# The last 64 rows of three weight matrices loaded in another shape, and two wo heads loaded apart

## The chip, the core and the metric

One core of one Trainium2 chip runs the kernel. The metric is the device time of one execution in microseconds; before the change three runs took 1284.09, 1285.81 and 1285.73 us (median 1285.73). The profile is of one further execution. A core has engines that run side by side, each with its own queue of instructions: TensorE (PE, with its weight loads shown as PEld), VectorE (DVE), ScalarE (ACT), GpSimd (POOL) and SyncE (SP), which here issues nearly all transfers. The transfers themselves run on 16 DMA engines. Engines wait for each other through semaphores.

## The reference, cut to what matters

One token of decoding: 16 query heads of 256 over 8 key/value heads with 65536 cached positions, a gated feed-forward block on the same x, and a mix of the two by a gate.

```python
x = A_x                                            # 1 x 1 x 448
g = sigmoid((x * gate_w).sum(-1, keepdims=True))
q = (x @ wq)                                       # wq 448 x 4096, 16 heads of 256
p = softmax(q . k / 16)                            # per head, over 65536 positions
o = p @ v                                          # two query heads share one k/v head
a = o.reshape(1, 1, 4096) @ wo                     # wo 4096 x 448
gate, up = x @ W_gate, x @ W_up                    # 448 x 1792 each
b = (gate * (gate > 0) * up) @ W_down              # W_down 1792 x 448
out = g * a + (1 - g) * b
```

All tensors are bfloat16. The K and V caches are 268 MB each, everything else together about 12 MB.

## The kernel before

A planner object collects operations (`op`), transfers (`dma`) and operations that use one shared PSUM bank (`mop`). Each has an engine, a key and the operations it depends on. `finish` sorts every engine's list by key, and that is the order in which the engine's queue runs; `emit` puts a semaphore wait in front of an operation for each dependency. A transfer counts as done when its semaphore has risen by 16, so a wait on it is for the whole transfer. The keys are estimated due times: `order` lists the loads in the order of issue with a length for each (`TILE` 19.35 for an 8.4 MB tile of K or V), and `tL` holds the running sum.

Loads go into three large SBUF buffers, `ring[0..2]`, in rotation. Each of the 8 k/v heads has four K tiles and four V tiles, 32 of each. The order is: wq and the main parts of W_gate and W_up, the last rows of wq, the first K tile, the last rows of W_gate and W_up, W_down, then K and V tiles in turn, V three tiles behind. Heads 0 to 2 of wo come after V tile 29, head 3 after V tile 30; the last V tile comes in four pieces (`PIECES`, half, quarter, eighth, eighth), and then heads 4, 5, 7 and 6 of wo, head 6 in two halves (`WOP`, L211). W_down and the second K tile wait until q is computed, because they overwrite wq's buffers.

A K tile is transposed by VectorE in eight pieces (L351), multiplied with q by TensorE (L363), reduced to a maximum by VectorE (L502) and exponentiated by ScalarE (L504). Behind the fourth tile of a head stand the maximum over all tiles, the rescaling (L524) and TensorE's transposes of the probabilities (L529). A V tile is multiplied by them (L397). When a head is complete, VectorE copies o (L411, L412), TensorE turns it into columns with eight small products (L420), VectorE scales them (L427), and `f_wo` (L594) multiplies them with that head's part of wo into one accumulator, eight products for a head. The last step copies the accumulator (L603) and stores it (L605).

A matrix of 448 rows doesn't fill 128 partitions evenly. The first 384 rows are loaded three to a partition in one transfer (wq L436, W_gate and W_up L450). `rows64` (L371) loads the last 64 rows of each of the three matrices: eight transfers of 6 rows (L374) on partitions 0 to 23 and 32 to 55 of one buffer, and four transfers of 4 rows (L377) on partitions 0 to 15 of a second one; the rows of one transfer lie four partitions apart. Partitions of the first buffer that hold no row are set to zero beforehand (`z_q` on VectorE, L243, for wq; `z_f` on GpSimd, L244, for the other two), and the transfers wait for it. x is brought into the matching arrangement by small products (`f_xT`, L289) and copies (`f_xT2`, L298); `xw` spreads it so that a product puts q of one head into one row of PSUM. `f_q` (L311) computes q from the first 384 rows; `f_q2` (L318) adds the last 64, with 16 products over 56 partitions (L320) and 16 over 16 (L323). `f_gu` (L454) and `f_gu2` (L464) do the same for W_gate and W_up, with 28 products over 56 partitions (L468) and 28 over 16 (L473) in `f_gu2`.

At the end the keys of the last wo products hang on `t7` (L587), the key of the last head's scaling L427: heads 4 and 5 get `t7 - 0.6`, ahead of the small products L420 (`t7 - 0.5`), the others `t7 + 0.6`.

Of the kernel before, what the change touches and what calls it, by code (L numbers as in the profile page):

```python
# [90 lines left out]
def bass_gated_mix__gqa_block_cached__glu_gated_reglu__decode_kernel(  # L91
# [13 lines left out]
    H = A_k_cache.shape[1]  # L105
# [13 lines left out]
    NX = R3 + 2  # L119
    KA = 48  # L120
    KB = D - NR3 - KA
# [6 lines left out]
    assert KR == 64 and KB == 16 and FT * 128 == F and FT <= 14 and FT % 2 == 0 and D <= 448 and H >= 3  # L128

    es = ExitStack()  # L130
    with es:
# [29 lines left out]
        xw = P_sb[:, 0:NX * 160]  # L161
        iot = P_sb[:, 800:1056].bitcast(I32)
        qn = P_sb[:, 1056:1312]
        x_row = P_sb[0:1, 1312:1312 + D]
        fin_o = P_sb[0:1, 0:D]
# [5 lines left out]
        wqa, wqb = ring[1][:, 0:NQ], ring[1][:, NQ:2 * NQ]  # L171
# [35 lines left out]
        for n in range(1, NT):  # L207
            order.append(("k", n, TILE))
            if n >= NTH - 1:
                order.append(("v", n - (NTH - 1), TILE))  # L210
        WOP = [[(0, 0, 4), (1, 0, 4), (2, 0, 4)], [(3, 0, 4)],  # L211
               [(4, 0, 4), (5, 0, 4), (7, 0, 4), (6, 0, 2), (6, 2, 4)]]
# [30 lines left out]
        z_q = op("dv", -0.5, lambda e: e.memset(wqa[0:32, :], 0.0))  # L243
        z_f = op("gp", -0.5, lambda e: e.memset(ring[2][0:32, R3 * NQ + 2 * R3 * F:R3 * NQ + 2 * R3 * F + 2 * F], 0.0))  # L244
        c_xT = op("dv", -0.3, lambda e: e.memset(xT[:], 0.0))
# [43 lines left out]
        def f_xT(e):  # L289
            for kt in range(R3):  # L290
                e.matmul(XT_ps[:, kt:kt + 1], x_row[0:1, kt:NR3:R3], one_t[0:1, 0:1], start=True, stop=True)
            for p0 in (0, 32):
                c0 = NR3 + (p0 // 32) * 24
                e.matmul(XT_ps[p0:p0 + 24, R3:R3 + 1], x_row[0:1, c0:c0 + 24], one_t[0:1, 0:1], start=True, stop=True)
            return e.matmul(XT_ps[0:KB, R3 + 1:NX], x_row[0:1, NR3 + KA:D], one_t[0:1, 0:1], start=True, stop=True)
        x1_ = mop("pe", 0.6, f_xT, [d_x, c_o1])

        def f_xT2(e):  # L298
            e.tensor_copy(xT[:, 0:R3], XT_ps[:, 0:R3])
            for p0 in (0, 32):  # L300
                e.tensor_copy(xT[p0:p0 + 24, R3:R3 + 1], XT_ps[p0:p0 + 24, R3:R3 + 1])
            return e.tensor_copy(xT[0:KB, R3 + 1:NX], XT_ps[0:KB, R3 + 1:NX])
        x2_ = mop("dv", 0.7, f_xT2, [x1_, c_xT])


        xw3 = xw.rearrange("p (kt c) -> p kt c", kt=NX)
        def f_xw(e):
            return e.tensor_copy(xw3[:, :, 31:160:32], xT[:].unsqueeze(2).to_broadcast([128, NX, 5])[:, :, 0:5])
# [9 lines left out]
        def f_q2(e):  # L318
            for j in range(J):
                e.matmul(QN_ps, xw3[0:56, R3, 31 - j:159 - j], wqa[0:56, j * 256:(j + 1) * 256],  # L320
# [323 lines left out]
```

## Time and profile before

| | us |
|---|---|
| three runs | 1284.09, 1285.81, 1285.73; median 1285.73 |
| the profiled execution | 1284.16 |
| its span, first to last instruction | 1282.9 |
| busy in it: VectorE | 638.9 (50%) |
| TensorE products | 430.9 (34%) |
| TensorE weight loads | 163.2 (13%) |
| ScalarE | 61.4 (5%) |
| GpSimd | 7.6 (1%) |

The profile divides the span into 40 equal slices and gives each engine's busy share in tenths, the share of the 16 DMA engines, and the rate at which they moved data. A group line gives line, engine, operation and tiles, the count, the total and mean time, and then the time the engine had stood idle before these instructions with what ended it. A timeline line gives start, length, engine, line, operation, tiles and count; the bracket at its end is the idle time ahead of it and its releaser. A line marked SPq is a transfer being issued, not its way through the DMA engines. A row of a table of windows gives start and end, the length, and for each of five engines busy time and (in brackets) count, then the clock granted to TensorE, the DMA share and GB/s. The lines on the sizes of transfers end with the time from issue to landing.

### The profile page before, as it was taken

What the parts mean: (1) busy time and instruction counts of PE and PEld (TensorE: products, weight loads), DVE (VectorE), ACT (ScalarE), POOL (GpSimd) and SP (SyncE); (2) the same over time, 40 slices, a digit from 0 to 9 for tenths busy, and PEclk for the clock granted to TensorE, in tenths of its full rate; (3) what the DMA queues carried; (4) which work ended last, traced back from release to release, by engine and by line L of the source; (5) the groups of instructions that cost most, each with busy time, mean ns of one, the idle gap of its engine ahead of it and who ended that gap; (6) DMA issues with size and microseconds to landing.
All of it is one profiled execution on the core that took longest, in us unless ns stands there. A gap on an engine that the chain in (4) does not pass through costs nothing.

```text
span 1282.9 us, 10059 instructions
## 1 busy us (share of the span) xinstructions
PE 430.9 (34%) x4649; PEld 163.2 (13%) x4649; DVE 638.9 (50%) x439; ACT 61.4 (5%) x116; POOL 7.6 (1%) x22
## 2 busy tenths in 40 slices
PE   5424423334223431225331343321433323233245
PEld 3301101111001110002110111100111101011011
DVE  2588633565434655445555444555434655335600
ACT  0000000000000000000000000000000000000000
POOL 2000000000000000000000000000000000000000
PEclk8665666656666666666656676656566656666566
DMA  9999999999999999999999999999999999999997
GB/s 413 436 426 430 438 434 426 438 435 432 428 434 436 436 430 429 432 444 426 426 440 438 425 434 440 428 425 438 440 426 430 436 439 426 436 430 438 432 399 317
DMA packets 11904, 549.68 MB, mean 428 GB/s; under 512 B 1427, under 2 KB 1686, under 8 KB 2710
## 3 DMA queue, kind: packets, MB, share of 16 engines
q1 hardware_dynamic: 11858, 549.03, 99.2%
q8 instruction: 36, 0.59, 0.2%
q14 instruction: 6, 0.05, 0.0%
q10 hardware_dynamic: 4, 0.00, 0.0%
HBM read 549.03 MB, written 0.00 MB: 428 GB/s over the span
## 4 chain that ended last, share of the span: by engine, by line
DVE 35%; DMA 31%; another core or an unknown queue 16%; PE 15%; SPq 2%; issue 1%; ACT 1%
DVE ring L351 31%; DMA ring<-in_A_k_cache_dram 27%; PE ST L363 6%; PE O L397 6%; DMA ring<-in_A_wo_dram 3%; DVE P_sb L524 1%; DMA ring<-in_B_W_up_dram 1%; SPq L374 1%; DVE nmb L502 1%; PE PT L529 1%; SPq L377 1%; ACT ptp L538 0%; PE M_ps L516 0%; DVE attnT L427 0%
## 5 line engine op out<-in xcount | busy, mean ns | idle before, releaser
L351 DVE STREAM_TRANSPOSE ring<-ring 128x2048 uint32<-128x2048 uint32 x256 | 565.5, 2275 | 405.8 <-DMA ring<-in_A_k_cache_dram 405.8
L363 PE MATMUL ST<-ring,xm 128*16 128x512 bf16 x2048 | 224.7, 612 | 755.7 <-DVE ring L351 755.7
L363 PEld LDWEIGHTS ST<-ring,xm 128*16 128x16 bf16 x2048 | 62.2, 120 | 904.3 <-DVE ring L351 796.2
L397 PE MATMUL O<-ring,ptp 128*4 128x512 bf16 x2048 | 150.9, 458 | 32.7 <-DMA ring<-in_A_v_cache_dram 28.7
L504 ACT ACTIVATE P_sb<-ST,nmb 128x512 bf16<-128x512 f32 x32 | 45.1, 1410 | 1107.8 <-DVE nmb L502 1107.8
L502 DVE TENSOR_REDUCE nmb<-ST 128x1 f32<-128x512 f32 x32 | 22.1, 689 | 109.3 <-PE ST L363 109.3
L397 PEld LDWEIGHTS O<-ring,ptp 128*4 128x4 bf16 x2048 | 54.9, 99 | 127.8 <-issue 60.4
L411 DVE CAST o_sb<-O 128x512 bf16<-128x512 f32 x8 | 5.5, 692 | 77.0 <-PE O L397 77.0
L524 DVE TENSOR_TENSOR P_sb<-P_sb,hs 128x1024 bf16<-128x1024 bf16 x16 | 18.9, 1222 | 8.7 <-ACT hs L518 8.7
L529 PE MATMUL PT<-identb,P_sb 128*128 128x128 bf16 x128 | 16.5, 310 | 15.5 <-DVE P_sb L524 14.7
L529 PEld LDWEIGHTS PT<-identb,P_sb 128*128 128x128 bf16 x128 | 12.3, 140 | 18.3 <-DVE P_sb L524 18.3
L538 ACT COPY ptp<-PT 128x256 bf16<-128x256 bf16 x32 | 10.4, 376 | 23.0 <-PE PT L529 23.0
L442 DVE STREAM_TRANSPOSE ptp<-P_sb 128x128 uint32<-128x128 uint32 x1 | 0.3, 311 | 18.3 <-ACT P_sb L441 18.3
L504 ACT ACTIVATION_READ_ACCUMULATOR P_sb<-ST,nmb 128x1 f32 x32 | 8.4, 262 | 0.0
L314 PE MATMUL M_ps<-ring,P_sb 128*128 128x256 bf16 x48 | 7.1, 322 | 0.8 <-DMA ring<-in_A_wq_dram 0.8
L427 DVE TENSOR_SCALAR attnT<-M_ps,hs 64x4 bf16<-64x4 f32 x16 | 3.5, 221 | 5.4 <-PE M_ps L420 5.3
L514 PE MATMUL M_ps<-identf,hs 128*2 128x128 f32 x8 | 2.6, 322 | 10.0 <-DVE hs L512 10.0
L598 PE MATMUL A_ps<-ring,attnT 128*1 128x224 bf16 x64 | 5.2, 322 | 1.7 <-DMA ring<-in_A_wo_dram 1.1
L314 PEld LDWEIGHTS M_ps<-ring,P_sb 128*128 128x128 bf16 x48 | 5.4, 115 | 2.3 <-DMA ring<-in_A_wq_dram 0.8
L460 PE MATMUL M_ps<-xT,ring 128*128 128x1 bf16 x84 | 5.2, 198 | 1.6 <-DVE nselT L445 1.6
L460 PEld LDWEIGHTS M_ps<-xT,ring 128*128 128x128 bf16 x84 | 5.1, 158 | 1.9 <-issue 1.9
L420 PE MATMUL M_ps<-emat,o_sb 128*128 128x2 bf16 x64 | 2.8, 166 | 7.0 <-DVE o_sb L412 7.0
(83 smaller groups left out, 85.9 us busy)
## 6 DMA issues: line engine op xcount, KB each, us to landing
ring<-in_A_v_cache_dram SPq DMA_DIRECT2D x1, 4096.0 KB, 27.4
ring<-in_A_wq_dram SPq DMA_DIRECT2D x1, 3072.0 KB, 10.0
ring<-in_A_v_cache_dram SPq DMA_DIRECT2D x1, 2048.0 KB, 32.0
ring<-in_A_v_cache_dram SPq DMA_DIRECT2D x2, 1024.0 KB, 35.0
ring<-in_B_W_down_dram SPq DMA_DIRECT2D x1, 1568.0 KB, 19.3
ring<-in_B_W_gate_dram SPq DMA_DIRECT2D x1, 1344.0 KB, 12.8
ring<-in_B_W_up_dram SPq DMA_DIRECT2D x1, 1344.0 KB, 15.6
ring<-in_A_wo_dram SPq DMA_DIRECT2D x1, 1344.0 KB, 20.9
```

The costliest lines, as they stand in the source:

```text
L314: ins = e.matmul(QN_ps, xw3[:, kt, 31 - j:159 - j], wq3[:, kt * NQ + j * 256:kt * NQ + (j + 1) * 256], start=(j == 0 and kt == 0), stop=Fa ...
L351: return lambda e: e.transpose(v, v)
L363: ins = e.matmul(bank[32 * w:32 * w + 16, :], xm[:, x0:x0 + 16], ktv[sl][:, u0:u0 + 16, c, :, r_], start=(b == 0 and c == 0 and r_ == 0), ...
L374: dma("sp", t + 0.0001 * i, sem, lambda e, b0=b0, r0=r0: e.dma_start(dst[b0:b0 + 21:4, :], W[r0:r0 + 21:4, :]), deps)
L377: d_ = dma("sp", t + 0.001 + 0.0001 * i, sem, lambda e, i=i: e.dma_start(dst2[i:i + 13:4, :], W[NR3 + KA + i:NR3 + KA + i + 13:4, :]), deps)
L397: ins = e.matmul(OP[h % 2][32 * g:32 * g + 4, :], ptp[h % 2][:, col:col + 13:4], ring[sl][:, k * 512:(k + 1) * 512], start=(a == 0 and k < ...
L460: ins = e.matmul(GU_ps[:, c:c + 1], wf3[which][:, kt * F + ft:(kt + 1) * F:FT], xT[:, kt:kt + 1], start=(c == 0 and kt == 0), stop=False, ...
L502: smax[n] = op("dv", tk + 22, lambda e, n=n, NM=NM, t_=t_: e.tensor_reduce(NM[:, t_:t_ + 1], ST[n % 2][:], AX.X, ALU.max, negate=True), [q ...
L504: aexp[n] = op("ac", tk + 23, lambda e, n=n, t_=t_, NM=NM, RS=RS: e.activation(P_sb[:, t_:2048:4], ST[n % 2][:], ACTF.Exp, bias=NM[:, t_:t ...
L524: rsc = op("dv", tt, lambda e, X=X, pb=pb: e.tensor_tensor(pb, pb, X[:, 12:16].unsqueeze(1).to_broadcast([128, 256, 4]), ALU.mult), [h7, a ...
L529: ins = e.transpose(PT[rd][:, s * 128:(s + 1) * 128], P_sb[:, (rd * 8 + s) * 128:(rd * 8 + s + 1) * 128], identb[:, :])
L538: ins = e.copy(dst, src)
```

## The change

The last 64 rows of wq are loaded by one transfer as 128 half rows of 2048 numbers: partition 2r + c holds half c of row r. It waits for no clearing. `f_q2` takes 16 products over 128 partitions; x is laid out for it twice, once with its values on the even partitions and zeros on the odd ones (heads in the first half), once the other way (second half). The last 64 rows of W_gate and W_up each go as 16 transfers of 4 rows, on partitions 0 to 15 and 32 to 47 of two buffers; both buffers are cleared on partitions 0 to 31 by GpSimd. `f_gu2` keeps 2 x 28 products, over 48 partitions each. x gets into its new arrangement by three small VectorE copies into a cleared row (`x_per`) ahead of the seven products of `f_xT`.

At the end heads 4 and 5 of wo are two transfers instead of one, and head 5's products get a key behind L420 (`t7 - 0.3`), ahead of those of heads 7 and 6.

```diff
-        z_q = op("dv", -0.5, lambda e: e.memset(wqa[0:32, :], 0.0))
-        z_f = op("gp", -0.5, lambda e: e.memset(ring[2][0:32, R3 * NQ + 2 * R3 * F:R3 * NQ + 2 * R3 * F + 2 * F], 0.0))
-        c_xT = op("dv", -0.3, lambda e: e.memset(xT[:], 0.0))
+        z_f = op("gp", -0.5, lambda e: e.memset(ring[2][0:32, WB - 2 * F:WB + 2 * F], 0.0))
+        c_xp = op("dv", -0.3, lambda e: e.memset(x_per, 0.0))
...
-            for p0 in (0, 32):
-                c0 = NR3 + (p0 // 32) * 24
-                e.matmul(XT_ps[p0:p0 + 24, R3:R3 + 1], x_row[0:1, c0:c0 + 24], one_t[0:1, 0:1], start=True, stop=True)
-            return e.matmul(XT_ps[0:KB, R3 + 1:NX], x_row[0:1, NR3 + KA:D], one_t[0:1, 0:1], start=True, stop=True)
-        x1_ = mop("pe", 0.6, f_xT, [d_x, c_o1])
+            for kt in range(4):
+                ins = e.matmul(XT_ps[:, R3 + kt:R3 + kt + 1], x_per[0:1, kt * 128:kt * 128 + 128], one_t[0:1, 0:1], start=True, stop=True)
+            return ins
+
+        def f_xp(e):
+            xr = x_row[0:1, NR3:D]
+            for c in range(2):
+                e.tensor_copy(x_per[0:1, 129 * c:129 * c + 127:2], xr)
+            return e.tensor_copy(x_per[0:1, 256:512].rearrange("o (b a r) -> o b a r", b=2, a=4)[:, :, 0:2, 0:16],
+                                 xr.rearrange("o (b a r) -> o b a r", b=2, a=2))
+        x0_ = op("dv", 0.5, f_xp, [d_x, c_xp])
+        x1_ = mop("pe", 0.6, f_xT, [d_x, c_o1, x0_])
...
-                e.matmul(QN_ps, xw3[0:56, R3, 31 - j:159 - j], wqa[0:56, j * 256:(j + 1) * 256],
-                         start=False, stop=False, skip_group_check=True)
-            for j in range(J):
-                ins = e.matmul(QN_ps, xw3[0:KB, R3 + 1, 31 - j:159 - j], wqb[0:KB, j * 256:(j + 1) * 256],
+                c, k = divmod(j, J // 2)
+                ins = e.matmul(QN_ps, xw3[:, R3 + c, 31 - j:159 - j], wqa[:, k * 256:(k + 1) * 256],
                                start=False, stop=(j == J - 1), skip_group_check=True)
...
-        def rows64(sem, t, dst, dst2, W, deps):
-            for i in range(8):
-                b0, r0 = i % 4 + 32 * (i // 4), NR3 + i % 4 + 24 * (i // 4)
-                dma("sp", t + 0.0001 * i, sem, lambda e, b0=b0, r0=r0: e.dma_start(
-                    dst[b0:b0 + 21:4, :], W[r0:r0 + 21:4, :]), deps)
-            for i in range(4):
-                d_ = dma("sp", t + 0.001 + 0.0001 * i, sem, lambda e, i=i: e.dma_start(
-                    dst2[i:i + 13:4, :], W[NR3 + KA + i:NR3 + KA + i + 13:4, :]), deps)
+        def rows64(sem, t, dsts, W, deps):
+            for i in range(16):
+                b0, r0 = i % 4 + 32 * (i // 4 % 2), NR3 + i % 4 + 16 * (i // 4)
+                d_ = dma("sp", t + 0.0001 * i, sem, lambda e, i=i, b0=b0, r0=r0: e.dma_start(
+                    dsts[i // 8][b0:b0 + 13:4, :], W[r0:r0 + 13:4, :]), deps)
             return d_
...
-                l_["wqh"] = rows64("wqh", t + 0.01, wqa, wqb, A_wq, [z_q])
+                l_["wqh"] = dma("sp", t + 0.01, "wqh", lambda e: e.dma_start(
+                    wqa, A_wq[NR3:D, :].rearrange("r (c n) -> (r c) n", c=2)))
...
-                    if runs and runs[-1][1] == h and (lo, hi) == (0, 4):
+                    if i < 2 and runs and runs[-1][1] == h:
...
-                    key = t7 + (-0.6 if h < H - 2 else 0.6) + 0.01 * k
+                    key = t7 + (-0.6 if h == H - 4 else -0.3 if h == H - 3 else 0.6) + 0.01 * k
```

31 lines of the change are left out of this document (14 added, 17 removed).

## The prediction

> **What bounds the kernel now.** I read the page first: the slices of the span, the DMA queues, the costliest groups.
>
> ```profile
> DMA  9999999999999999999999999999999999999997
> ...
> DMA packets 11904, 549.68 MB, mean 428 GB/s; under 512 B 1427, under 2 KB 1686, under 8 KB 2710
> ...
> q8 instruction: 36, 0.59, 0.2%
> ...
> L351 DVE STREAM_TRANSPOSE ring<-ring 128x2048 uint32<-128x2048 uint32 x256 | 565.5, 2275 | 405.8 <-DMA ring<-in_A_k_cache_dram 405.8
> ```
>
> The 16 DMA engines are busy in all 40 slices at 428 GB/s, so one engine moves 428/16 = 26.75 GB/s. VectorE's transposes of K sat idle for 405.8 us, all of it put down to the arrival of K. The kernel lasts as long as its 549.68 MB take; what can shorten it is a better share-out among the 16 engines, and the work behind the last bytes. So I read the windows where the stream ends:
>
> ```profile
> 1224.00:1228.00 4.00, 3.19 (x40) 0.98 (x32) 0.00 (x0) 0.00 (x0) 0.00 (x0) 0.74 0.57 239
> 1260.00:1272.00 12.00, 5.46 (x48) 1.32 (x48) 0.00 (x0) 0.00 (x0) 0.00 (x0) 0.65 0.97 406
> ...
> 1276.00:1277.00 1.00, 0.01 (x2) 0.02 (x4) 0.82 (x2) 0.00 (x0) 0.00 (x0) 0.50 0.12 50
> 1277.00:1278.00 1.00, 1.00 (x12) 0.70 (x14) 0.00 (x0) 0.00 (x0) 0.00 (x0) 0.50 0.13 50
> ```
>
> The column before the last is the DMA share. From 1276 to 1278 it is 0.12 to 0.13, which is two engines of 16: the others are done, and the end waits for these two. At 1224 to 1228 it had already fallen to 0.57: engines that were ahead had used up what was issued. So some engines carry more than others. The timeline of the start shows why; the brackets give the idle time before a line and what ended it.
>
> ```profile
> 3.00 5.79 SPq L374 DMA_DIRECT2D ring<-in_A_wq_dram  x8
> 8.83 2.49 SPq L377 DMA_DIRECT2D ring<-in_A_wq_dram  x4
> ...
> 10.79 7.14 PE L314 MATMUL M_ps<-ring,P_sb 128*128 128x256 bf16 x48 [0.76 <-DMA ring<-in_A_wq_dram]
> 11.37 0.47 SPq L496 DMA_DIRECT2D ring<-in_A_k_cache_dram  x1
> ...
> 21.07 3.49 PE L320 MATMUL M_ps<-ring,P_sb 56*128 56x256 bf16 x16 [3.15 <-DMA ring<-in_A_wq_dram]
> ...
> 40.35 6.70 DVE L351 STREAM_TRANSPOSE ring<-ring 128x2048 uint32<-128x2048 uint32 x3 [9.90 <-DMA ring<-in_A_k_cache_dram]
> 44.74 1.81 PE L468 MATMUL M_ps<-xT,ring 56*128 56x1 bf16 x28 [8.96 <-DMA ring<-in_B_W_up_dram]
> ```
>
> In order of issue: wq's main part, the main parts of W_gate and W_up, wq's last rows, the first K tile, the last rows of W_gate and W_up. The first K tile lands at 40.35, the last W rows at 44.74. In these 4.39 us come 2 x 64 rows of 3584 B = 458,752 B, which is 104 GB/s, a quarter of 428. The last rows run on some four engines, while the others go on to W_down and the second K tile. Likewise wq's last rows (524,288 B): the main parts of W, 2 x 1344 KB (row below) or 2.75 MB, need 6.4 us after 10.8, and 21.07 is 3.9 us later, 136 GB/s, about a third of the full rate. Whoever carries these rows is behind from then on and stays behind to the end.
>
> **The change part by part.** Sizes and counts of the issues that change:
>
> ```profile
> ring<-in_B_W_gate_dram SPq DMA_DIRECT2D x1, 1344.0 KB, 12.8
> ...
> ring<-in_A_wo_dram SPq DMA_DIRECT2D x1, 896.0 KB, 37.6
> ...
> ring<-in_A_wq_dram SPq DMA_DIRECT2D x8, 48.0 KB
> ring<-in_B_W_gate_dram SPq DMA_DIRECT2D x8, 21.0 KB
> ...
> ring<-in_A_wq_dram SPq DMA_DIRECT2D x4, 32.0 KB
> ring<-in_B_W_gate_dram SPq DMA_DIRECT2D x4, 14.0 KB
> ```
>
> Before, each matrix's 64 rows go as 8 transfers of 6 rows and 4 of 4 rows. I take it that each row of a transfer goes to another engine and that each transfer begins at the same first engine; the quarter and the third of the rate agree. Then four engines carry 8 + 4 = 12 rows of each matrix, two carry 8, ten carry none.
>
> wq's rows. Before: 12 rows of 8192 B on the loaded engines, 98,304 B / 26.75 GB/s = 3.67 us. After: one transfer over 128 partitions, 8 half rows of 4096 B on each of 16 engines, 1.22 us on all. The loaded engines gain 2.45 us; the others lose 1.22, but they are ahead by more. Bounds for a half row: 0.153 us by the rate, 0.21 by the price per byte of the interval from 40.35 to 44.74, so the gain is 2.45 to 2.0.
>
> W_gate's and W_up's rows. Before 24 rows on each of the four engines; after 16 transfers of 4 rows each, all on four engines: 32 rows. A row costs 0.134 us by the rate (3584 B) and at most 4.39/24 = 0.183 us by that interval, which also holds a semaphore's way. Eight more rows cost 1.07 to 1.46 us; I take 1.15, near the rate, since the interval holds more than the rows.
>
> Together the loaded engines are 2.45 - 1.15 = 1.3 us earlier (0.55 to 1.4), and everything that waits for whole tiles with them: each K and V tile, and the last pieces.
>
> The queue of SP, and what hides the rest:
>
> ```profile
> 0.72 3.07 POOL L244 MEMSET ring<- 32x3584 bf16 x1 [0.29 <-POOLq L629]
> ...
> 1.21 1.76 DVE L243 MEMSET ring<- 32x2048 uint32 x1 [1.21 <-PEq L629]
> ...
> 20.12 5.63 SPq L374 DMA_DIRECT2D ring<-in_B_W_up_dram  x8
> ...
> 25.79 2.50 SPq L377 DMA_DIRECT2D ring<-in_B_W_up_dram  x4
> ...
> 28.34 0.44 SPq L483 DMA_DIRECT2D ring<-in_B_W_down_dram  x1
> 28.82 0.43 SPq L496 DMA_DIRECT2D ring<-in_A_k_cache_dram  x1
> ```
>
> A 4-row issue costs 2.50/4 = 0.63 us. wq's single transfer waits for no clearing (VectorE's 1.76 us is gone), so the first K tile is issued at about 2.6 rather than 11.37. Then SP stands at GpSimd's clearing, twice as wide now, 2 x 3.07 = 6.1 us, done at 6.9; behind it 32 issues x 0.63 = 20 us, so W_down and the second K tile go out at 27 to 27.5 (before 28.34 and 28.82). The clearing also delays GpSimd's constants by 3 us; their first reader (L444) comes only behind q's second part. The engines without extra rows hold bytes till 40.35 minus the loaded ones' 2.45 + 1.22, about 37: the clearing and the issues are hidden by 10 us. If that cover were gone, each us would count in full. The second part of q takes 16 products over 128 partitions in place of 32; 3.5 us go, hidden, since W_down and K wait for SP. VectorE's small copies of x stand ahead of the first products, but those wait for wq until 10.79 and VectorE has 1.76 us less to clear, so: nothing. The products of W's last rows stay 2 x 28, and end about 1.3 earlier with their landing.
>
> **The end**, from the timeline:
>
> ```profile
> 1274.86 1.02 PE L397 MATMUL O<-ring,ptp 128*4 128x512 bf16 x8 [1.45 <-DMA ring<-in_A_v_cache_dram]
> 1275.93 0.69 DVE L411 CAST o_sb<-O 128x512 bf16<-128x512 f32 x1 [54.83 <-PE O L397]
> 1276.54 0.28 DVE L412 CAST o_sb<-O 128x128 bf16<-128x128 f32 x1
> ...
> 1276.98 1.65 PE L598 MATMUL A_ps<-ring,attnT 128*1 128x224 bf16 x16 [1.10 <-DMA ring<-in_A_wo_dram]
> ...
> 1278.57 0.37 PE L420 MATMUL M_ps<-emat,o_sb 128*128 128x2 bf16 x8
> 1278.98 0.46 DVE L427 TENSOR_SCALAR attnT<-M_ps,hs 64x4 bf16<-64x4 f32 x2 [2.16 <-PE M_ps L420]
> ...
> 1279.58 1.66 PE L598 MATMUL A_ps<-ring,attnT 128*1 128x224 bf16 x16 [0.64 <-DVE attnT L427]
> ...
> 1281.28 0.38 DVE L603 CAST P_sb<-A_ps 1x224 bf16<-1x224 f32 x1 [1.84 <-PE A_ps L598]
> ```
>
> Let L be 1274.86, when the last V piece is there. Its products and the two copies of o end at L+1.96 (1276.82). The 8 small transposes of o (L420) could go, but on TensorE the 16 products of heads 4 and 5 stand ahead, and these wait for their 896 KB until L+2.12 and take 1.65. So L420 starts at L+3.71, VectorE scales (0.46), the last 16 products end at L+6.38 (1281.24).
>
> After: the last wo transfer falls into head 4, head 5, head 7 and the halves of head 6, each head 448 KB, that is 1.06 us (half of 2.12). They land at L+1.06, 2.12, 3.18, 3.71 and 4.24. A product costs 1.65/16 = 0.103 us. Head 4's 8 products, the only ones ahead of L420, run from L+1.06 to 1.89: they cost nothing as long as the copies take until 1.96. L420 then goes at L+2.0, scaling is done at 2.9; in that time head 5's products run, 2.4 to 3.2. Head 7: 3.2 to 4.05. Head 6: 4.05 to 4.9, each half after its landing. End at L+4.9, a gain of 1.45. Bounds: the last half's landing and its 4 products, L+4.65, gain 1.7; if head 5's products ran only after the scaling, 24 products from 2.97, L+5.45, gain 0.9. The next thing late is then the last landing itself. The additional issue on SP is hidden:
>
> ```profile
> L580 SPq DMA_DIRECT2D ring<-in_A_wo_dram x6: 387/957/10032, 1213.8 to 1251.4; - x6
> ```
>
> One of these issues took 10.03 us, the queue having no room, and the last began at 1251.4; one more of that kind would be out by 1265, ahead of the windows from 1272 on in which wo comes.
>
> Sum: -1.3 - 1.45 = -2.75 us (-1.45 to -3.1). The profiled execution took 1284.16 (span 1282.9 and 1.3 around it), so it would take 1281.4. The three runs shown are 1284.09, 1285.73 and 1285.81: the profile is of the lower level, and from the median 1285.73 the sum gives 1283.0. Nothing in the change chooses the level; I say 1282.2, between the two.
>
> **The rivals.**
>
> *Only the end gains.* Who is last isn't set by these rows alone: the 36 instruction fetches of 16 KB also pass through single engines, each 16,384 / 26.75 GB/s = 0.6 us at least. If they fall one or two more on a loaded engine than before, the 1.3 us are used up: 1284.16 - 1.45 = 1282.7. For it: two engines are last, not four, so something beside the rows matters. Against: the count of instructions, and so of fetches, hardly changes.
>
> *Only the rows gain*, because the products at the end don't overlap with landings as I place them: 1284.16 - 1.3 = 1282.9. Against: each order and landing above has its row.
>
> *4-row transfers are dear, and it gets slower.* Place: the 32 transfers on the four engines. If the 6-row transfers' rows went at the rate (16 x 0.134 = 2.14 us of the 4.39), the eight 4-row ones before took 2.25, 0.281 each. Then 32 cost 9.0, +4.6, against 2.45 and 1.45 gained: 1284.16 + 0.7 = 1284.9. It decides from a price of (4.39 + 3.9) / 32 = 0.26 us per row; 2.6 us slower needs 0.34. Against: both kinds end in rows of the same 3584 B, and wq's 12 transfers came at 3.9 us where the rate alone makes 3.67. [...]
>
> *The change doesn't do what it says: wq's half rows don't spread over 16 engines.* Were they on four, each had 32 x 0.153 = 4.9 us instead of 1.22, so +3.7: 1285.1, slower too. Against: the tiles of 128 partitions, K and V, move at 428 GB/s, on all 16. [...]
>
> *The queue of SP jams.* 32 waiting transfers could fill it as at 1241; if W_down and the second K tile went out only after the first K tile is through, at some 40 instead of 27, the engines without extra rows would stand for 3 to 4 us, about their lead: 1282 to 1284. Against: before, 24 waiting transfers let K out in 0.43 us.
>
> **How the numbers follow.** Forecast 0.62; only the end 0.14; only the rows 0.08; dear 4-row transfers 0.09; not spread 0.03; jam 0.04. What a measurement of this kernel can tell from no change is about 0.2%, 2.6 us; against the median 1285.73 that is 1283.2. The forecast lies below it but for one part in eight (the upper level with a small sum): 0.54. The two half gains and the jam fall on both sides, 0.06 of 0.26 below. So faster 0.60, same 0.31, slower 0.09 from the dear and unspread rows. The range: low end 1281.4 less the rest of the bounds, 0.4, and 1 us for a better turn of the fetches, 1280.0; high end the half gains at the upper level, 1285.73 - 1.3 = 1284.4, and some of the dear case: 1284.9.
>
> **What would show it.** q's second part starts near 18.5 instead of 21.07; the first K tile lands at 37 to 38 instead of 40.35; W's last rows come 4.3 us or more behind it, 5.9 at most by my bounds, beyond 8 the dear rival. W_down is issued at 27 to 27.5. At the end L420 follows the copies of o at once, with 8 products ahead of it, and last products and last landing lie within 0.8 us. L itself is 1.3 earlier. I am wrong if L doesn't move, if L420 still waits for wo, or if the DMA share at the end shows four or more engines late together.

## The result and the profile after

| | before | changed |
|---|---|---|
| median, us | 1284.98 (6 runs, 1284.09 to 1285.81) | 1281.03 (6 runs, 1281.02 to 1281.17) |
| profiled execution, us | 1284.16 | 1281.17 |
| its span, us | 1282.9 | 1279.9 |

The ratio is 0.997, its 95% interval 0.9959 to 0.998. Before has two levels, about 1284.2 and 1285.7, that come almost in turn; the changed kernel has one. Profiled execution against profiled execution, 2.99 us are gone.

The page of the changed kernel: the slices of the DMA engines, the packets, the instruction fetches, the transposes of K.

```profile
DMA  9999999999999999999999999999999999999997
...
DMA packets 11936, 549.68 MB, mean 429 GB/s; under 512 B 1395, under 2 KB 1654, under 8 KB 2806
...
q8 instruction: 36, 0.59, 0.2%
...
L352 DVE STREAM_TRANSPOSE ring<-ring 128x2048 uint32<-128x2048 uint32 x256 | 565.5, 2275 | 408.9 <-DMA ring<-in_A_k_cache_dram 408.9
```

The same 549.68 MB at 429 GB/s: it is still the stream that sets the time. The timeline of the start:

```profile
0.72 6.06 POOL L243 MEMSET ring<- 32x7168 bf16 x1 [0.29 <-POOLq L628]
...
2.11 0.75 SPq L435 DMA_DIRECT2D ring<-in_A_wq_dram  x1
...
2.90 0.44 SPq L495 DMA_DIRECT2D ring<-in_A_k_cache_dram  x1
...
6.80 10.04 SPq L375 DMA_DIRECT2D ring<-in_B_W_gate_dram  x16
...
10.99 8.35 PE L317 MATMUL M_ps<-ring,P_sb 128*128 128x256 bf16 x48 [0.65 <-DMA ring<-in_A_wq_dram]
...
16.88 9.86 SPq L375 DMA_DIRECT2D ring<-in_B_W_up_dram  x16
...
19.40 1.92 PE L324 MATMUL M_ps<-ring,P_sb 128*128 128x256 bf16 x16
...
26.79 3.03 SPq L482 DMA_DIRECT2D ring<-in_B_W_down_dram  x1
29.86 4.93 SPq L495 DMA_DIRECT2D ring<-in_A_k_cache_dram  x1
38.79 6.70 DVE L352 STREAM_TRANSPOSE ring<-ring 128x2048 uint32<-128x2048 uint32 x3 [15.10 <-DMA ring<-in_A_k_cache_dram]
43.51 1.81 PE L467 MATMUL M_ps<-xT,ring 48*128 48x1 bf16 x28 [14.50 <-DMA ring<-in_B_W_up_dram]
```

The second part of q (L324) no longer waits for its rows; the first K tile lands 1.56 us earlier, the last W rows 1.23 us earlier and 4.72 us behind K. SP waits for GpSimd's clearing until 6.8, and two issues stand still, 3.03 and 4.93 us, behind the 32 small transfers.

The timeline of the end, and then the windows of the end:

```profile
1273.30 1.03 PE L395 MATMUL O<-ring,ptp 128*4 128x512 bf16 x8 [1.45 <-DMA ring<-in_A_v_cache_dram]
...
1274.36 0.91 PE L597 MATMUL A_ps<-ring,attnT 128*1 128x224 bf16 x8
...
1274.98 0.28 DVE L410 CAST o_sb<-O 128x128 bf16<-128x128 f32 x1
...
1275.32 0.38 PE L418 MATMUL M_ps<-emat,o_sb 128*128 128x2 bf16 x8
...
1275.63 2.63 PE L597 MATMUL A_ps<-ring,attnT 128*1 128x224 bf16 x24
1275.74 0.46 DVE L425 TENSOR_SCALAR attnT<-M_ps,hs 64x4 bf16<-64x4 f32 x2 [0.47 <-PE M_ps L418]
...
1278.30 0.38 DVE L602 CAST P_sb<-A_ps 1x224 bf16<-1x224 f32 x1 [2.10 <-PE A_ps L597]
```

```profile
1260.00:1272.00 12.00, 5.35 (x56) 1.33 (x56) 0.00 (x0) 0.00 (x0) 0.00 (x0) 0.76 0.95 393
...
1275.00:1276.00 1.00, 0.94 (x18) 0.56 (x16) 0.51 (x4) 0.00 (x0) 0.00 (x0) 0.50 0.31 124
1276.00:1277.00 1.00, 0.94 (x12) 0.38 (x10) 0.19 (x1) 0.00 (x0) 0.00 (x0) 0.50 0.27 103
```

L is 1273.30 for 1274.86, 1.56 earlier. The last products end at 1278.26, L+4.96 for L+6.38: 1.42 more. Together 2.98 of the 2.99 us. The share of 0.27 to 0.31 is four to five engines of 16, where two were late before.

**What the packets tell.** The trace also holds a record of each DMA packet: start, length, size, queue, but no engine. In before 7455 of the 7486 packets of 3584 B or more that start between 60 and 1190 us do so 3 to 4 ns before another one's recorded end; I take it that such a packet follows that one on the same engine, so an engine's history can be followed backwards; where two engines end within 1 to 2 ns, the link is doubtful. Times of packets are counted here and in the table below from a moment 0.35 us before the timeline's zero. I look at the moment at which each engine leaves V tile 29 (packets of 65,536 B) for wo's heads 0 to 2 (3584 B), its turn. In each of the fourteen profiles L comes 43.6 to 43.8 us after the latest turn. Worked out from the packets of before:

```
turns: 1220.1 1220.2 1220.6 1225.6 1226.0 1226.3 1226.3 1226.3 1226.9 1227.5 1227.8 1227.9 1227.9 1227.9 1230.95 1231.19
the one at 1231.19: 12 packets of 8192 B, 24 of 3584 B at the start, no 16 KB fetch;
                    8 KB fetches at 54.2, 420.4, 808.4, 1196.4
1227.5, 1227.8, 1227.9: also 36 rows, no 16 KB fetch
1230.95: 16 KB fetches at 144, 450, 739, 1024; its rows can't be followed
changed kernel: latest turns 1229.0, 1229.23, 1229.71
the one at 1229.71: 16 KB fetches at 917.0 and 1223.3
the one at 1229.23: 8 KB fetch at 807.5; the next of this kind comes at 1277.1
```

So the latest in the kernel before is one of the four engines with 12 + 24 rows, as the prediction had it. Three things were not in the prediction. Only one of these four is last, as it also carries four of the six 8 KB fetches (a second queue of the page, `q14 instruction: 6`): each takes 0.31 us and stretches the packet behind it from 2.42 to 3.08, nearly 1 us apiece, and its fellows turn 3.3 to 3.7 us earlier. The 36 fetches of 16 KB go round over only eight of the other engines (each gets every eighth, some 300 us apart) and cost 1.0 to 1.1 us plus 0.5 us for the stretched neighbour; so those turn some 5.5 us or more behind the three that carry nothing. And one of these eight turned only 0.24 us before the last; from its place, 3 to 5 us behind its fellows, I take it for one of the two with 8 + 16 rows. The other of the two is then the engine at 1225.6, on which no 16 KB fetch is found: its rows (4.71 us) put it about where it stands.

In the changed kernel the last is another one. The engine that turned at 1229.71 has 16 KB fetches at 917.0 and 1223.3, with no doubtful link on the way back to them: it is one of the eight. The engine with the 8 KB fetch at 807.5, also without a doubtful link, turned at 1229.23, 1.96 us earlier than in the kernel before. Not all of this is the rows: the fetch that came at 1196.4 before comes only at 1277.1 here, after the turn, so this engine is spared about 1 us that the change did not set out to save. Why it comes later no run shows.

### The profile page after: what moved, and what is told of

Its sections match the earlier page's. It is cut to its first block, busy times and chain, and to the rows that moved or that the text cites. A ratio compares the mean times of both kernels' runs of the same rounds, so it can differ in the third digit from the quotient of the medians.

```text
span 1279.9 us, 10025 instructions
## 1 busy us (share of the span) xinstructions
PE 426.5 (33%) x4634; PEld 159.5 (12%) x4634; DVE 639.1 (50%) x438; ACT 61.5 (5%) x116; POOL 10.5 (1%) x22
## 2 busy tenths in 40 slices
DMA packets 11936, 549.68 MB, mean 429 GB/s; under 512 B 1395, under 2 KB 1654, under 8 KB 2806
## 4 chain that ended last, share of the span: by engine, by line
DVE 34%; DMA 31%; another core or an unknown queue 16%; PE 14%; SPq 2%; issue 1%; ACT 1%; POOL 0%; POOLq 0%
DVE ring L352 31%; DMA ring<-in_A_k_cache_dram 27%; PE ST L364 6%; PE O L395 6%; DMA ring<-in_A_wo_dram 3%; DVE P_sb L523 1%; SPq L375 1%; DMA ring<-in_B_W_up_dram 1%; DVE nmb L501 1%; PE PT L528 1%; POOL ring L243 0%; ACT ptp L537 0%; PE M_ps L515 0%; DVE attnT L425 0%
## 5 line engine op out<-in xcount | busy, mean ns | idle before, releaser
L364 PE MATMUL ST<-ring,xm 128*16 128x512 bf16 x2048 | 225.5, 614 | 754.0 <-DVE ring L352 754.0
L243 POOL MEMSET ring<- 32x7168 bf16 x1 | 6.1, 6061 | 0.3 <-POOLq L628 0.3
```

Source lines behind the costliest of these rows:

```text
L243: z_f = op("gp", -0.5, lambda e: e.memset(ring[2][0:32, WB - 2 * F:WB + 2 * F], 0.0))
L364: ins = e.matmul(bank[32 * w:32 * w + 16, :], xm[:, x0:x0 + 16], ktv[sl][:, u0:u0 + 16, c, :, r_], start=(b == 0 and c == 0 and r_ == 0), ...
```

## The experiments

All but e2 are made from the changed kernel; e2 is made from the kernel before. A time is given with its ratio to the kernel before and the ratio's 95% interval. First the two halves of the change, one at a time.

**e1**: the loads of the start as changed, the end as before.

```diff
-               [(H - 4, 0, 4), (H - 3, 0, 4), (H - 1, 0, 4), (H - 2, 0, 2), (H - 2, 2, 4)]]
+               [(4, 0, 4), (5, 0, 4), (7, 0, 4), (6, 0, 2), (6, 2, 4)]]
...
-                    if i < 2 and runs and runs[-1][1] == h:
+                    if runs and runs[-1][1] == h and (lo, hi) == (0, 4):
...
-                    key = t7 + (-0.6 if h == H - 4 else -0.3 if h == H - 3 else 0.6) + 0.01 * k
+                    key = t7 + (-0.6 if h < H - 2 else 0.6) + 0.01 * k
```

> The change's loads at the start, with the end as before (heads 4 and 5 of wo in one transfer, their 16 products ahead of L420). L is the start of the products of the last V piece: 1274.86 before, 1273.30 after the change. Theory (the end waits for the few DMA engines that carry the last rows; fewer bytes on them move L): L 1273.3, the last wo product ends at L+6.4, execution 1282.5 to 1282.7. Rival A (L moved because of where instruction fetches fell, not because of the rows): L anywhere between 1273 and 1276, not the same as after the change, execution 1282.5 to 1285.7. Rival B (nothing but the end counts): 1284.1.

1282.46 (ratio 0.9981, 0.9972 to 0.9989), one level. L is 1273.16, the last products end at L+6.44.

**e2**: the other way round, the start as before with the changed end.

```diff
-               [(4, 0, 4), (5, 0, 4), (7, 0, 4), (6, 0, 2), (6, 2, 4)]]
+               [(H - 4, 0, 4), (H - 3, 0, 4), (H - 1, 0, 4), (H - 2, 0, 2), (H - 2, 2, 4)]]
...
-                    if runs and runs[-1][1] == h and (lo, hi) == (0, 4):
+                    if i < 2 and runs and runs[-1][1] == h:
...
-                    key = t7 + (-0.6 if h < H - 2 else 0.6) + 0.01 * k
+                    key = t7 + (-0.6 if h == H - 4 else -0.3 if h == H - 3 else 0.6) + 0.01 * k
```

> The loads at the start as before, with the change's end (heads 4 and 5 apart, head 5 behind L420). Theory: L stays at 1274.9, the last product ends at L+4.95 instead of L+6.38, execution 1282.6 to 1282.8 for the lower level of the kernel before and 1284.2 for its upper one. Rival (the end gains only because the rows bring wo earlier): L+6.4, 1284.1. If the two levels of the kernel before (1284.1 and 1285.7) come from the start, they are here too; if they come from the end, they are gone.

1282.84 (0.9986, 0.9977 to 0.9995), in two levels, about 1282.8 and 1284.2. L is 1275.06, the end L+4.85. The two halves are separate and add up: the end is worth 1.45 on either level of before, and the two levels belong to the old start.

**e3**: wq as half rows, but W_gate's and W_up's rows again in transfers of 6 and 4.

```diff
...
-            for i in range(16):
...
+            for i in range(8):
+                b0, r0 = i % 4 + 32 * (i // 4), NR3 + i % 4 + 24 * (i // 4)
+                dma("sp", t + 0.0001 * i, sem, lambda e, b0=b0, r0=r0: e.dma_start(
+                    dsts[0][b0:b0 + 21:4, :], W[r0:r0 + 21:4, :]), deps)
+            for i in range(4):
...
```

> As after the change, but the last rows of W_gate and W_up go again as 8 transfers of 6 rows and 4 of 4 rows: 24 rows on each loaded engine, not 32. Theory: the change's 4-row transfers cost 1.1 to 1.2 us, so L comes at 1272.1 and the execution takes 1279.8 to 1280.0. Rival (4-row and 6-row transfers cost the same in sum, since what counts is all rows of a matrix): 1281.0, L 1273.3.

1282.97 (0.9979, 0.997 to 0.9988), levels at about 1281.6 and 1283.0: a miss, slower than the changed kernel.

```profile
1275.22 1.02 PE L399 MATMUL O<-ring,ptp 128*4 128x512 bf16 x8 [1.44 <-DMA ring<-in_A_v_cache_dram]
```

The row is the timeline's last group of products of the last V piece, so L; this profile is of the upper level. By the sum L should have come 2.45 before 1274.86.

**e4**: W_gate's and W_up's rows as half rows too, one transfer each over 128 partitions.

```diff
...
-                    a2.append(rows64("wfh%d" % i_, t + 0.1 + 0.1 * i_, (wfa[i_], wfb[i_]), W, [z_f]))
+                    a2.append(dma("sp", t + 0.1 + 0.1 * i_, "wfh%d" % i_, lambda e, W=W, i_=i_: e.dma_start(
+                        wfa[i_][:, 0:F // 2], W[NR3:D, :].rearrange("r (c f) -> (r c) f", c=2))))
...
```

> As after the change, but the last rows of W_gate and W_up also go as half rows on 128 partitions, one transfer each; 56 products as before, each over 128 partitions into 64 outputs. No DMA engine carries more than another. Theory: 32 rows of 0.134 to 0.143 us on the loaded engines (4.3 to 4.6 us) give way to 1.1 us on all: L 3.2 to 3.5 us earlier, 1270.0, execution 1277.6 to 1277.9. Rival (once the rows are level, the engines that carry the instruction fetches are last, or the issue of the last V tiles bounds): gain 1 to 2 us, 1279 to 1280. Rival (1792 B per partition is dear): no gain or a loss, 1281 or more.

1282.07 (0.9976, 0.9967 to 0.9986), L at 1274.46. Another miss: with all rows spread evenly it is 1.0 us slower than the changed kernel. From the turns in e4 (seven engines from 1222.4 to 1223.3, eight from 1228.7 to 1230.9) I saw the eight engines with fetches, and formed a new theory: these alone set the end, rows on the first four cost nothing, and 4-row transfers help by taking the rows off the two engines that carry both. The next four runs test it against the prediction's own account.

**e5**: wq as before, W rows four at a time. **e6**: wq's rows four at a time as well.

```diff
...
-                l_["wqh"] = dma("sp", t + 0.01, "wqh", lambda e: e.dma_start(
-                    wqa, A_wq[NR3:D, :].rearrange("r (c n) -> (r c) n", c=2)))
+                l_["wqh"] = rows64("wqh", t + 0.01, (wqa, wqb), A_wq, [z_q])
...
```

(e6; e5 has before's eight transfers of 6 rows and four of 4 in this place.)

> As after the change (its end too), but wq's last rows go as before: 8 transfers of 6 rows, 4 of 4. W_gate's and W_up's stay 4 at a time. Old theory (the four engines with most rows set the end): 12 rows of wq instead of 8 half rows on them, +2.45, execution 1283.5. New theory (eight of the 16 DMA engines also carry the instruction fetches and are 6 to 8 us behind for that alone; the two engines that take the 5th and 6th row of a 6-row transfer are among them, the first four are not; last is whoever has the largest sum): the two have 8 rows of wq (2.45) where after the change they have 8 half rows (1.22), the first four have 3.7 + 4.4 = 8.1 without fetches, so the end lies 0 to 1.2 behind that of the change: 1281.0 to 1282.3.

> As after the change, but wq's last rows too go 4 at a time: 16 rows of 8192 B (4.9 us) and 32 of 3584 B (4.4 us) on the first four engines, none on the others. Old theory: the four are 3.7 us later than after the change, 1284.7. New theory: the fetch engines lose their 1.2 us, the four stand at 9.3 against about 8 to 8.5 for the last fetch engine after the change: +0.8 to +1.3, 1281.8 to 1282.3, and one level, since the last engines carry no fetches.

e5: 1284.14 (0.9992, 0.9983 to 1.0001), e6: 1285.19 (1.0001, 0.9992 to 1.001). Both go against the new theory; e5 is 0.6, e6 0.5 from the old one. In e6 something came on top: all sixteen engines were slow in two stretches, in the second and third of these windows

```profile
14.00:16.00 2.00, 2.00 (x12) 1.34 (x11) 0.00 (x0) 0.00 (x0) 0.00 (x0) 1.00 1.01 430
16.00:20.00 4.00, 4.00 (x34) 3.28 (x32) 0.00 (x0) 0.00 (x0) 0.00 (x0) 1.00 0.99 344
...
36.00:38.00 2.00, 0.00 (x0) 0.00 (x0) 0.00 (x0) 0.00 (x0) 0.00 (x0) 0.50 0.81 233
```

**e7**: half of wq's half rows on the first four engines, issued by ScalarE.

```diff
...
+                l_["wqh0"] = dma("sp", t + 0.01, "wqh", lambda e: e.dma_start(wqa[0:64, :], wqs[0:64, :]))
+                for i_ in range(16):
+                    b0 = 64 + i_ % 4 + 16 * (i_ // 4)
+                    l_["wqh"] = dma("ac", -7 + 0.01 * i_, "wqi", lambda e, b0=b0: e.dma_start(
+                        wqa[b0:b0 + 13:4, :], wqs[b0:b0 + 13:4, :]))
...
```

> As after the change, but of wq's 128 half rows 64 go in one transfer over 16 engines (4 each, 0.6 us), and 64 in 16 transfers of 4, issued by ScalarE, on the first four engines (16 each, 2.4 us). Old theory: the four are 1.8 us later, 1282.9. New theory: the fetch engines are 0.6 us earlier, the four (0.6 + 2.4 + 4.4 = 7.4) still not last: 1280.4, faster than the change.

1286.99 (1.0014, 1.0005 to 1.0023), beyond both. ScalarE issued its rows from 1.55 to 12.16 us, while SP's packets of 24,576 to 65,536 B were under way; the rows were there only at 33.4, and W_down was issued only at 37.02: in e7's timeline

```profile
37.02 0.61 SPq L486 DMA_DIRECT2D ring<-in_B_W_down_dram  x1
```

The engines were slow besides (320 GB/s from 20 to 24 us). As a test of the theory it says nothing.

**e8**: the products of q and K in two half widths each, 2048 products and as many weight loads more, and so more fetches, at the same work.

```diff
-                            ins = e.matmul(bank[32 * w:32 * w + 16, :], xm[:, x0:x0 + 16], ktv[sl][:, u0:u0 + 16, c, :, r_],
...
+                            for hf in range(2):
+                                ins = e.matmul(bank[32 * w:32 * w + 16, 256 * hf:256 * hf + 256], xm[:, x0:x0 + 16],
+                                               ktv[sl][:, u0 + 8 * hf:u0 + 8 * hf + 8, c, :, r_],
...
```

> As after the change, but each product of q with K is made as two of half the width: 2048 products and 2048 weight loads more, 16 more instruction fetches of 16 KB (52 instead of 36), the same bytes of K and V. TensorE has the room (33% busy). New theory: two fetches more on each of eight engines, 1.07 us each at least: L 2.1 to 3.0 us later, execution 1283.1 to 1284.0. Old theory, or fetches that pass beside the data: L as after the change within 0.3, 1281.0 to 1281.3 plus what the last products lose (below 0.3).

1284.05 (0.9993, 0.9984 to 1.0001), L at 1276.16, 2.86 later. The page's line of the fetches and the group of the products:

```profile
q8 instruction: 52, 0.85, 0.3%
...
L365 PE MATMUL ST<-ring,xm 128*16 128x256 bf16 x4096 | 227.2, 409 | 754.6 <-DVE ring L352 754.6
```

TensorE waits for K as long as before (754.6 for 754.0 us), and two fetches more fall on each of the eight engines: their time is real, about 1.5 us each. Here, in e4 and in the changed kernel itself, these engines are the last. That explains e4: its half rows of W_gate and W_up put 1.18 us on every engine (2.45 of rows in the table below, less 8 of 0.159), and its latest turn is 1.14 us behind the changed kernel's.

**e9**: W_gate's and W_up's rows in pairs, 8 transfers of 4 x 7168 B per matrix on partitions 0 to 31, which need no clearing by GpSimd. **e10**: the same, with half of wq's half rows in 4-partition transfers on SP.

```diff
...
-            for i in range(16):
-                b0, r0 = i % 4 + 32 * (i // 4 % 2), NR3 + i % 4 + 16 * (i // 4)
...
+            src = W[NR3:D, :].rearrange("(p k) f -> p (k f)", k=2)
+            for i in range(8):
+                b0 = i % 4 + 16 * (i // 4)
+                d_ = dma("sp", t + 0.0001 * i, sem, lambda e, b0=b0: e.dma_start(
+                    dsts[b0:b0 + 13:4, :], src[b0:b0 + 13:4, :]), deps)
...
+                dma("sp", t + 0.01, "wqh", lambda e: e.dma_start(wqa[0:64, :], wqs[0:64, :]))
+                for i_ in range(16):
+                    b0 = 64 + i_ % 4 + 16 * (i_ // 4)
+                    l_["wqh"] = dma("sp", t + 0.011 + 0.0001 * i_, "wqh", lambda e, b0=b0: e.dma_start(
+                        wqa[b0:b0 + 13:4, :], wqs[b0:b0 + 13:4, :]))
```

> The changed kernel, with the last 64 rows of W_gate and W_up two to a partition on 32 partitions: 8 transfers of 4 partitions x 7168 B per matrix in place of 16 of 4 x 3584 B. The same bytes go through the same first four DMA engines, with half the DMA issues on SP and no clearing on GpSimd. Theory of the fetches (the end is set by the most lagging of the engines that carry instruction fetches, and none of those carries a row of W_gate or W_up here): the same as the changed kernel, about 1281.0, between 1279.5 and 1282.5 as the fetches fall. Rival (the queue of SP, which stood still for 3 to 5 us at the start behind many small transfers, costs time at the end): 0.5 to 1.5 us faster than the changed kernel at an unchanged spread of the engines, with the first K tile and the first packets of K tile 1 earlier by as much.

> The kernel of e9, with 64 of the 128 half rows of wq in 16 transfers of 4 partitions, all on SP: 4.4 us of engine time is put on the first four DMA engines' side instead of being spread over all sixteen, so that those four carry some 7.4 us beside K and V and the other twelve 0.6 us less than in e9. It is e7 without ScalarE's queue. Theory of the fetches (four engines without fetches have 6 to 8 us to spare at the end): not slower than e9, 1280.4 if the fetches fall alike, at most 1281.5. Rival, the prediction's own account (the loaded four engines set the end): 1.5 to 2 us slower than e9, about 1282.9. If the first packets of K tile 1 come later than in e9 on all engines, the difference is the queue's and neither is told.

e9: 1283.49 (0.9984, 0.9975 to 0.9993); e10: 1288.01 (1.0021, 1.0012 to 1.003). Neither is what either theory said, and since K tile 1 starts later in e10, its time alone decides nothing. The windows of 38 to 46 us, the changed kernel and then e9:

```profile
38.00:46.00 8.00, 2.50 (x42) 2.53 (x43) 6.70 (x3) 0.00 (x0) 0.00 (x0) 0.50 1.19 501
```

```profile
38.00:46.00 8.00, 0.59 (x10) 0.62 (x11) 6.68 (x3) 0.00 (x0) 0.00 (x0) 0.50 1.08 310
```

All sixteen engines are busy, at 310 GB/s for 501 (a packet counts whole where it starts): a packet of K took up to 3.80 us for 2.42, one of W_down 0.97 for 0.47. But the order of the turns decides: in e10 one engine turns at 1236.87, 2.7 us behind all others, and it has no 16 KB fetch. It is one of the first four, which by the new theory had time to spare. That theory falls here as a rule for all kernels; for the changed kernel itself it names the right engines.

**e11**: wq's half rows read one behind the other, W's pairs into adjoining partitions. **e12**: e9's transfers cut into two of 3584 B per partition. The two edits are shown against e10 and against e9.

```diff
-                        wqa[b0:b0 + 13:4, :], wqs[b0:b0 + 13:4, :]))
+                        wqa[b0:b0 + 13:4, :], wqs[64 + 4 * i_:68 + 4 * i_, :]))
...
-                    dsts[b0:b0 + 13:4, :], src[b0:b0 + 13:4, :]), deps)
+                    dsts[4 * i:4 * i + 4, :], src[b0:b0 + 13:4, :]), deps)
```

```diff
-            for i in range(8):
-                b0 = i % 4 + 16 * (i // 4)
+            for i in range(16):
+                b0, c0 = i % 4 + 16 * (i // 4 % 2), i // 8 * F
...
-                    dsts[b0:b0 + 13:4, :], src[b0:b0 + 13:4, :]), deps)
+                    dsts[b0:b0 + 13:4, c0:c0 + F], src[b0:b0 + 13:4, c0:c0 + F]), deps)
```

> The kernel of e10 with its two sets of small transfers laid out otherwise, the same bytes on the same engines. In e10 the packets of all sixteen engines ran slow in two stretches: while wq's half rows landed (16.5 to 24 us: 205 to 300 GB/s for 430 before) and while W_gate's and W_up's pairs landed (43 to 50 us: 259 to 338 GB/s). Both sets read DRAM at a distance from one engine to the next (16384 B, 28672 B) and write partitions 4 apart. Here wq's half rows are read one behind the other (4096 B from engine to engine) into the same partitions 4 apart; the pairs are read as in e10, into 4 adjoining partitions. Theory of the reading (the distance in DRAM makes the conflict): the first stretch is gone (over 400 GB/s from 17 to 24 us), the second stays; about 2.6 us faster than e10, 1285.4. Theory of the writing (partitions 4 apart): the first stays, the second is gone; about 2.4 us faster, 1285.6. If both stay (1288.0), neither is the cause, and what slows all engines stays open; if both go (1283.0), it is the two together.

> The kernel of e9, with each transfer of 4 partitions x 7168 B cut into two of 4 partitions x 3584 B: the same bytes from the same addresses to the same partitions, on the same four engines, but the packet size and the number of transfers (16 per matrix) of the changed kernel. What is open after e9 to e11 is what made all sixteen engines slow while the pairs landed (38.5 to 45 us: 212 to 338 GB/s). If it is the size of the packets or the few, large transfers, the stretch is gone (over 400 GB/s) and the time is that of the changed kernel, about 1281.0, to 1281.6 if the spread of the engines is that of e9. If it is where the bytes lie in DRAM or in SBUF, the stretch stays and the time is e9's, 1283.5.

e11: 1288.82 (1.0029, 1.0019 to 1.0039), e12: 1283.7 (0.999, 0.9981 to 0.9999). Both stretches stayed in e11, and the one in e12:

```profile
16.00:24.00 8.00, 4.06 (x32) 3.21 (x31) 0.00 (x0) 0.00 (x0) 0.00 (x0) 0.98 1.07 307
```

```profile
38.00:46.00 8.00, 0.68 (x12) 0.71 (x13) 6.13 (x3) 0.00 (x0) 0.00 (x0) 0.50 1.13 361
```

So it is neither the distance in DRAM nor that in partitions by itself, and not the size or number of the transfers. Nor is it that SP issues them earlier without the clearing (from 3.2 us on in e9 and e12, from 6.80 in the changed kernel): in e10 they go out from 13.24 on and are slow all the same. What is left is where the bytes lie, in DRAM or in SBUF. The rows' own packets, sixteen at a time in the order in which they started, show more:

```
median length, ns      partitions 0-15   16-31   0-15   16-31
e9   (7168 B)                272           533     428     498
e10  (7168 B)                272           510     316     540
e12  (3584 B)                140           140     232    176, once more 238, 168, 248, 171
changed (3584 B, 0-15 and 32-47): 140 six times, then 156, 174
```

In e9 and e10 the rows that the first four engines write to partitions 16 to 31 are the slow ones, and the lengths fall again in between, if not always to 272. wq's rows on 64 to 127 (e7, e10, e11) were slow too: e10 and e11 moved 307 GB/s from 16 to 24 us, e7 320 from 20 to 24 us, the changed kernel 469 from 16 to 24 us. In e12 the medians are the other way round: the first rows on 16 to 31 are slow only from the fourteenth of the sixteen on, so if these partitions are the cause, it acts a dozen packets late. That the partitions count fits e11, whose first sixteen pairs went to partitions 0 to 15, four adjoining ones to a transfer, and took 309 ns, little over 272. It does not fit e6, which was slow with all its rows on partitions 0 to 15 and 32 to 47 (344 and 233 GB/s in the windows above). No run put e9's pairs on partitions 0 to 15 and 32 to 47. Why all sixteen engines slow down together stays open.

**The sum over all runs.** With packets of 0.309 us (8192 B), 0.140 (3584 B), 0.159 (4096 B) and 0.272 (7168 B), the time of the rows on the first four engines is known for each kernel; the time lost to slow packets from 10 to 60 us is the sum of what they take beyond their usual length, over 16 engines, less that of before (0.23). The column "8 KB" counts how many of the fetches near 54, 420, 808 and 1197 us come before the turn; each one fewer than in before is counted as 0.97 us less (0.31 + 3.08 - 2.42). Starting from 1231.19 and 7.07 us, for the engine of the first four that has these fetches:

```
kernel   rows   slow  8 KB  worked out  latest turn   L        latest is
before   7.07   -      4    -        1231.19   1274.86   first four
e2       7.07   0      4    1231.2      1231.32   1275.06   not told apart
changed  5.75   0.07   3    1229.0      1229.71   1273.30   16 KB fetches
e1       5.75   0.05   3    1229.0      1229.55   1273.16   16 KB fetches
e5       8.19   0.21   4    1232.5      1232.53   1276.27   first four
e6       9.42   1.35   3    1233.9      1233.43   1277.13   first four
e7       7.66   3.54   3    1234.4      1235.07   1278.76   not followed
e9       5.62   2.87   4    1232.6      1232.91   1276.56   first four
e10      7.53   5.05   4    1236.7      1236.87   1280.49   first four
e11      7.53   5.59   4    1237.2      1237.36   1280.96   first four
e12      5.75   2.36   4    1232.2      1232.35   1276.04   not told apart
e3       4.63   0.05   4    1228.8      1231.57   1275.22   16 KB fetches
e4       2.45   0      3    1225.6      1230.85   1274.46   16 KB fetches
e8       5.75   0.18   3    1229.1      1232.38   1276.16   16 KB fetches
```

Of the ten kernels between before and e3, the sum comes within 0.3 us of the latest turn in e2, e5, e9, e10, e11 and e12, and e6 is 0.5 off. In the changed kernel and in e1 the engine with the 8 KB fetches turned at 1229.23 and, less surely followed, 1229.26, within 0.3 us of the sum, and an engine with 16 KB fetches came behind it. e7, whose last engine can't be followed, is 0.7 off. "First four" rests on the links: in before and e5 all four 8 KB fetches and the rows are found on the latest engine, in e6, e9, e10 and e11 one to three of these fetches; in e2 and e12 only the turn agrees. In e3 the engine with the four 8 KB fetches turns at 1228.87, as worked out; but two engines with 16 KB fetches turned later, at 1229.60 and 1231.57. That is where e3's gain went: the sum was right for its engine, and the engine was no longer the last. None of the twelve beats the changed kernel.

## Why the prediction was right

- *Which engines are last.* Right for the kernel before: four have 12 rows of each matrix, and the last is one of them; which one, the 8 KB fetches choose. "Two engines" of the window were, by the turns, this one and one with 16 KB fetches, which turned 0.24 us earlier. In the changed kernel it no longer holds: there the last is an engine with 16 KB fetches.
- *wq's half rows, -2.45.* 1231.19 to 1228.87 in e3 is -2.32. A half row took 0.159 us, the rate's 0.153.
- *Rows four at a time, +1.15.* 1231.19 to 1232.53 in e5 is +1.34, of which 0.21 are slow packets. What the prediction didn't see is that this loss buys something: it takes these rows off two more engines, and one of the two carries 16 KB fetches and was next in line. With its rows there, e3's L came 0.36 later than before's instead of 2.45 earlier (upper level against lower; e3's own lower level would be some 1.4 better). The edit that was costed as a loss is needed for the other's gain.
- *Together -1.3.* The latest turn came 1.48 earlier, L 1.56, and that this is so near is partly luck. The rows did what they were costed at: -2.32 (e3) and +1.13 (e5 without the slow packets) make -1.2. But the engine with the rows was also spared an 8 KB fetch, about 1 us, which the prediction didn't know of, and turned 1.96 earlier; then an engine with 16 KB fetches, 0.48 us behind it, took 0.48 of this away. With the fetch where it was, I estimate a turn of 1229.9 (the sum with four fetches) to 1230.2 (1229.23 + 0.97), which is 1.0 to 1.3 earlier than before.
- *The end, -1.45.* -1.42 in the profile, -1.45 in e2. Each step came as placed: head 4's products beside the copies, L418 0.06 us behind the copies, 24 products without a long gap, the end at L+4.96 for L+4.9.
- *The start.* Q's second part at 19.40 for 18.5 (its first part took 8.35 us for 7.14), K at 38.79 for 37 to 38, the clearing 6.06 for 6.1, W_down at 26.79 for 27. That SP would be held up behind 32 waiting transfers was a rival; it was, for 8 us in two issues (3.03 and 4.93), and it lay hidden as argued: K's last bytes came at 38.79.
- *The levels.* The sum gave 1281.4 from the profile's own time, 1281.17 came. The forecast of 1282.2 put half of an upper level on it, and the changed kernel has none. The two levels are 1.5 us apart, one 16 KB fetch. That before's upper level is one fetch more on the engine 0.24 us behind fits e2 and e3, which keep the 6-row transfers of W_gate and W_up and have two levels, and e1, e4 and e5, which do not and have one; it was only argued.
- *A bad sign.* The prediction named four or more engines late together as a mark of its being wrong. The windows show just that, 0.27 to 0.31, since the two last engines were brought level with the next ones: the three latest turns lie within 0.7 us. A gain from an even share-out must look so.
- *The rivals.* Only the end gains, because fetches fall elsewhere: one did, but off the loaded engine instead of onto it. Dear 4-row transfers: 0.140 us a row, not 0.26. Half rows not spread: L324 could start at 19.40. Only half a gain: e1 and e2 show both.

## What to carry to other kernels

Where the stream is the bound, work out the load of each DMA engine, with its fetches, and rank them: relieving the last is worth only its lead over the second, and an edit that looks like a loss on the first may be what relieves the second. Test the halves of a change one at a time, and look for the engine in the packets before giving up a sum: e3 and e4 seemed to refute this one, and only showed another engine behind it. Do the same where the sum and the time agree: in the changed kernel they agree although another engine is last. When small transfers are packed onto few engines, watch the GB/s while they land (310 from 38 to 46 us in e9, 501 in the changed kernel); whether other partitions would help e9's pairs was not tested.

## What was not expected of the hardware

- 36 fetches of 16 KB, 0.2% of the engines' time by the page, go over eight of the 16 engines and hold each up by about 1.5 us apiece, 6 us in all by the end of the stream; 16 more of them cost 3.0 us (e8). In this kernel, bound by its DMA engines, the time is not hidden: L came 2.86 us later in e8.
- While the first four engines loaded rows to partitions 0 to 31, all sixteen engines fell from about 430 to as little as 212 GB/s (half-microsecond windows of the packet records of e9); the cause is open.
- A transfer of 4 rows takes SP 0.63 us to issue (16 in 10.04 us). Behind 32 of them in the changed kernel the issue of the next large transfer took 3.03 us and of the one after it 4.93, for 0.44 and 0.43 in the kernel before, behind 24. In e5, where the 32 went out 5 us later, the next large one took 0.44.
